# Step stores interleaved by blocks of four steps, a pipelined end of the forward loop, the last output gradients moved into the O projection, and the epilogue into the Wo gradient

## The chip, the cores and the metric

One core of one Trainium2 chip. The time is the device time of one execution in microseconds (us). Four executions of the kernel before agree within 0.3%. A ratio is the mean time of one kernel's fast runs over that of the other's fast runs of the same rounds, with a 95% interval; it is therefore not quite the ratio of the medians that stand beside it.

## The reference, cut to what matters

The kernel computes the value and all gradients of `x + s * g` in bfloat16, for 2048 tokens of width 640. `s` is a recurrent attention with 32 heads of 128: 64 steps of 32 tokens, each with 8 memory rows that are the output of the step before. `g` is the silu of a gated MLP.

```python
for s in range(n_seg):                       # 64 steps
    h = jnp.concatenate([mem, xs], axis=1)   # 8 memory rows and 32 token rows
    q, k, v = [jnp.einsum('btd,dhe->bhte', h, W) for W in (Wq, Wk, Wv)]
    p = _softmax(jnp.where(mask, scores(q, k), -1e9))
    o = jnp.einsum('bhte,hed->btd', jnp.einsum('bhqk,bhke->bhqe', p, v), Wo)
    mem = o[:, :M, :].copy()                 # the recurrence
...
return x + s * g                             # then jax.vjp of all of it
```

## The kernel before: the parts that the change and the argument touch

Only the 8 memory rows of a step hang on the step before. So the forward loop runs a chain of 64 steps on 32 or 40 rows, and puts the attention of whole *tiles* into its gaps: a tile is three steps' memory rows (24) and 96 token rows, 120 rows in all. A *unit* is one tile and four heads (512 columns). The backward loop is built the same way from the end. What a step computes for its rows (q, v, k, and in the backward loop gO) goes to a *step store* in DRAM, and tiles are loaded from there:

```python
self.QVS = mk("QVS", (T, 4, 32, 2, 1024))          # step, head group, row, q or v, column
self.KS  = mk("KS",  (T, 4, 32, 1024))
self.GOS = mk("GOS", (T, 4, 32, 1024))

def step_src(self, w, t0, t1, r0, r1, c0, c1):      # x rows: t1 - t0 = 4, r0:r1 = 8:32
    ...
    return XS[t0:t1, g, r0:r1, c0 - 1024 * g:c1 - 1024 * g]   # [4 steps, 24 rows, columns]
```

The first 672 token rows come from other stores (QVX, KX), whose rows are evenly spaced. The end of the forward loop, the tail, works off the units that are left when the chain has ended. It fills the gaps of steps that no longer exist:

```python
for t in range(T, 3 * k.NTL + 4):
    for g in ("W0", "W1", "W2", "G1", "G2", "G3", "G4", "G5", "G6"):
        FILL(g, t, ...)
```

After it come the O projection (with the fetch of three transposed weights, of copies QM of the memory rows, and the epilogue that makes out0 and gz), the last output gradients GX0 as a phase of their own, and the prologue of the backward loop. Each unit of the attention weight gradients, which follow the backward loop, makes eight loads:

```python
nc.sync.dma_start(dS[0:n, :, 0:n], k.DSR[tl][:, h0:h0 + 4, :])
nc.sync.dma_start(Pr[0:n, :, 0:n], k.PR[tl][:, h0:h0 + 4, :])
for nm_ in ("g", "q", "k"):
    k.load_x(r, nm, src, nc.scalar if nm_ == "g" else nc.sync)                       # 96 x rows
    (nc.sync if nm_ == "k" else nc.scalar).dma_start(r[0:nm, :], k.m_src(...))       # 24 memory rows
```

## Time and profile before

The median is 5976.96 us (three runs, 5975.18 to 5979.66).

| stage, from its tiles' starts and ends | us before |
|---|---|
| MLP forward and start | 619.3 |
| forward loop | 1340.9 |
| tail of the forward loop | 101.9 |
| O projection, then GX0, with the hand-overs | 207.9 |
| prologue of the backward loop | 107.8 |
| backward loop | 1304.7 |
| attention weight gradients, with their start | 1605.4 |
| load before the Wo gradient | 54.2 |
| Wo gradient | 176.4 |
| w2 gradient | 82.3 |
| rest of the MLP gradients | 377.8 |

The next rows are the kernel before's busy times in the long stretches: forward loop, backward loop, weight gradients, Wo gradient. The columns are the stretch, its length, busy time and instructions of each engine, the granted TensorE clock, the mean busy share of the 16 DMA engines, and GB/s.

```profile
core 0: us, PE busy (x) PEld busy (x) DVE busy (x) ACT busy (x) POOL busy (x), PEclk, DMA share, GB/s
620.00:1960.00 1340.00, 1211.98 (x22292) 733.70 (x22413) 744.67 (x2174) 699.11 (x2397) 526.15 (x733) 0.98 0.50 144
2378.00:3683.00 1305.00, 1136.69 (x24059) 756.15 (x24180) 588.80 (x2766) 380.47 (x1226) 408.36 (x747) 0.91 0.59 161
3710.00:5288.00 1578.00, 1441.79 (x11404) 927.96 (x11404) 446.30 (x958) 379.56 (x616) 0.00 (x0) 0.95 0.33 89
5342.00:5518.00 176.00, 175.97 (x1278) 125.94 (x1278) 13.42 (x30) 11.30 (x30) 0.00 (x0) 0.99 0.47 150
```

TensorE is idle for 128, 168 and 136 us in the three loops and not at all in the Wo gradient. No mean DMA share comes near 1 (0.33 to 0.59). The Pool is idle in the last two rows.

### The profile page before, as it was taken

Reading aid. Unit: us, or ns where it says so; the run is one execution under the profiler, and the core shown is the slowest. Engines: PE = TensorE matmul, PEld = TensorE weight load, DVE = VectorE, ACT = ScalarE, POOL = GpSimd, SP = SyncE. Lnnn points to the kernel's source line nnn. Section 1 sums busy time; section 2 is a strip of 40 time slices with the busy share of each in tenths; the row PEclk is TensorE's granted clock in tenths of the full one; section 3 lists DMA queues with packets and bytes.
Section 4 is the critical chain, followed back from the end, with each engine's and each line's share of the span. In section 5 each row is a group of like instructions: output and inputs, shape, how many; then the busy total and the mean of one; then the engine's idle time right before and its main releaser. Section 6 shows DMA issues by size and latency. Waiting matters only on the chain. (4 is left out here: it accounts for less than half of the span.)

```text
span 5978.5 us, 165521 instructions
## 1 busy us (share of the span) xinstructions
PE 5060.8 (85%) x67367; PEld 3238.0 (54%) x67644; DVE 2395.6 (40%) x7482; ACT 1840.4 (31%) x5059; POOL 1045.7 (17%) x1647
## 2 busy tenths in 40 slices
PE   5969799989988464888888886899999999969899
PEld 2546455555555242555555664665566556637565
DVE  5724455555555233444444442332233222300351
ACT  2424355555545212332222331221223222200110
POOL 0000244344444301333333331000000000000000
PEclk9979899999999686998889997999999999989999
DMA  6465355555444764665555664433233323353342
GB/s 222 160 249 195 102 154 155 148 149 150 146 138 142 217 191 118 158 171 165 160 164 166 181 175 108 108 83 84 76 96 89 89 79 86 101 204 122 106 123 92
DMA packets 999893, 839.75 MB, mean 140 GB/s; under 512 B 476653, under 2 KB 891561, under 8 KB 995817
## 3 DMA queue, kind: packets, MB, share of 16 engines
q1 hardware_dynamic: 771860, 580.65, 33.4%
q0 software_dynamic: 52080, 122.53, 7.1%
q10 hardware_dynamic: 175193, 125.97, 7.0%
q8 instruction: 533, 8.73, 0.6%
q14 instruction: 227, 1.86, 0.1%
HBM read 511.81 MB, written 327.01 MB: 140 GB/s over the span
## 5 line engine op out<-in xcount | busy, mean ns | idle before, releaser
L1405 PE MATMUL wg<-gr,hr 120*128 120x512 bf16 (+1 forms) x2640 | 592.9, 386 | 17.1 <-DVE dST L1337 12.6
L1383 PE MATMUL g<-w,gT 128*128 128x320 bf16 x3840 | 560.5, 304 | 0.0
L1383 PEld LDWEIGHTS <-gT 128*128 128x128 bf16 x3840 | 374.2, 99 | 143.4
L1405 PEld LDWEIGHTS <-hr 120*128 120x128 bf16 (+1 forms) x2640 | 258.7, 99 | 343.2 <-issue 51.8
L1773 POOL TENSOR_TENSOR o<-gxn,ln_G 128x640 bf16<-128x640 f32 x16 | 22.3, 1396 | 2130.9 <-DVE gxn L1771 2130.9
L366 PEld LDWEIGHTS <-gkv 128*8 128x8 bf16 x8192 | 213.3, 98 | 154.4 <-DVE gkv L1054 34.2
L90 DVE CAST wgo<-wg 128x512 bf16<-128x512 f32 x72 | 47.5, 688 | 588.1 <-PE wg L1405 315.6
L347 PEld LDWEIGHTS <-hx 128*32 128x32 bf16 x7680 | 178.0, 96 | 164.9 <-issue 5.1
L90 DVE CAST stg<-bank 128x512 bf16<-128x512 f32 x256 | 177.1, 692 | 200.6 <-PE bank L347 190.4
L1350 ACT CAST gr<-r6p 120x512 bf16<-120x512 f32 (+1 forms) x176 | 102.9, 585 | 495.0 <-PE r6p L1347 231.8
L366 PE MATMUL gbank<-WvT,gkv 128*8 128x320 bf16 x4096 | 227.6, 398 | 27.0 <-DVE gkv L1054 27.0
L652 ACT ACTIVATE xP<-xsp,xnm 120x120 bf16<-120x120 f32 (+1 forms) x704 | 239.8, 376 | 8.9 <-DMA PR<-xP 3.2
L1392 DVE TENSOR_TENSOR ghacc<-ghacc,g 128x320 f32<-128x320 f32 x240 | 117.0, 488 | 291.1 <-PE g L1383 291.1
L92 ACT CAST wgo<-wg 128x512 bf16<-128x512 f32 x48 | 25.8, 589 | 640.1 <-PE wg L1405 640.1
L1493 PE MATMUL oa<-gow,orr 128*128 128x320 bf16 x1280 | 176.4, 301 | 54.2 <-DMA gow<-GWO 54.2
L663 POOL TENSOR_TENSOR xP<-xP,xrz 120x480 bf16<-120x480 bf16 (+1 forms) x176 | 170.0, 966 | 162.8 <-ACT xP L652 95.6
L1189 DVE SCALAR_TENSOR_TENSOR gdS<-gdp,Dx,gPr 120x120 bf16<-120x120 f32 (+1 forms) x704 | 188.8, 331 | 0.0
L92 ACT COPY gT<-t6g 128x960 bf16<-128x960 bf16 (+5 forms) x216 | 167.2, 794 | 60.7 <-PE t6g L1366 59.3
L529 DVE COPY vt<-stg 8x512 bf16<-8x512 bf16 x512 | 162.8, 318 | 51.4 <-ACT stg L92 44.0
L1493 PEld LDWEIGHTS <-orr 128*128 128x128 bf16 x1280 | 126.1, 99 | 104.6 <-issue 54.6
L1161 POOL DMA_DIRECT2D VTD<-gvT x176 | 129.4, 736 | 289.0 <-ACT gvT L1160 265.1
L1186 DVE CUSTOM_DVE_ANT_0 gdS<-gdp,gPr 120x120 bf16<-120x120 f32 (+1 forms) x704 | 153.7, 274 | 59.5 <-PE gdp L1175 58.4
(326 smaller groups left out, 10716.3 us busy)
## 6 DMA issues: line engine op xcount, KB each, us to landing
QVS<-stg SPq DMA_DIRECT2D x128, 256.0 KB
gqv<-QVS SPq DMA_DIRECT2D x112, 192.0 KB
vTt<-VTD SPq DMA_DIRECT2D x64, 320.0 KB
orr<-OR SPq DMA_DIRECT2D x16, 1280.0 KB
OR<-xv POOLq DMA_DIRECT2D x168, 120.0 KB, 3.2
VTD<-gvT POOLq DMA_DIRECT2D x168, 120.0 KB, 4.6
PR<-xP POOLq DMA_DIRECT2D x168, 112.5 KB, 4.5
gPr<-PR SPq DMA_DIRECT2D x168, 112.5 KB
```

The lines of the kernel that those rows point to most:

```text
L90: return nc.vector.tensor_copy(out, in_)
L92: return nc.scalar.copy(out, in_)
L347: k.nc.tensor.matmul(bank[32 * g:32 * g + 32, :], x[:, dc, :], W[:, dc, c0:c0 + 512], start=(dc == 0), stop=(dc == k.DC - 1), tile_positio ...
L366: k.nc.tensor.matmul(pm[p0:p0 + nq, 0:320], x[:, h, :], W[:, h, 320 * b:320 * b + 320], start=(first and i == 0), stop=(last and i == 15), ...
L529: nc.vector.tensor_copy(vt[p0:p0 + 8, c0:c0 + 512], sv[32 * g:32 * g + 8, b * 512:(b + 1) * 512])
L652: nc.scalar.activation(Pb[0:n, j, 0:n], sp[0:n, j, :], ACT.Exp, bias=nmx[0:n, j:j + 1], scale=k.scale, accum_out=Z[0:n, j:j + 1])
L663: nc.gpsimd.tensor_tensor(Pb[0:n, :, 0:n], Pb[0:n, :, 0:n], bc_last(rz[0:n], n), ALU.mult)
L1186: nc.vector.tensor_tensor_reduce(dS[0:n, j, :], dp[0:n, j, :], Pr[0:n, j, :], 1.0, 0.0, ALU.mult, ALU.add, Dx[0:n, j:j + 1])
L1189: nc.vector.scalar_tensor_tensor(dS[0:n, j, :], dp[0:n, j, :], Dx[0:n, j:j + 1], Pr[0:n, j, :], op0=ALU.subtract, op1=ALU.mult)
L1383: nc.tensor.matmul(pg[:], ring[:, i, j, r0:r0 + P], Ws[qd][i][:, j, 320 * h:320 * h + 320], start=(i == 0 and j == 0), stop=(i == 2 and j ...
L1405: nc.tensor.matmul(accs[dc][:], hr[0:n, tl, dc * P:(dc + 1) * P], st["g", NTL * qd + tl, i][0:n, :], start=(tl == 0), stop=(tl == NTL - 1))
L1493: nc.tensor.matmul(ac[j][i][:], orr[:, w, jj * P:(jj + 1) * P], gow[:, w, 320 * i:320 * i + 320], start=(w == 0), stop=(w == NW - 1))
```

## The change

Its intent is to make the x rows of a tile one evenly spaced block of DRAM, so that their load keeps more DMA engines busy (in the kernel before, in stretches of the weight gradients in which hardly any packets but those of the step-store loads are in flight, such as 4761 to 4762 and 4766 to 4767 us, the DMA share is 0.26 and 0.27, about four of 16; it is 0.94 from 4757 to 4758, where the loads of dS and P run too); to take idle time out of the stretches between the loops; and to move what fills no gap there (the epilogue of out0) to where engines are idle. The memory rows of a tile now straddle blocks of four steps and are loaded in one or two pieces, in the weight gradients by the Pool. In the prologue, part of each unit's loads move to the ACT queue. Small copies out of the store FS move from the O projection into the backward loop.

```diff
-        self.QVS = mk("QVS", (T, 4, 32, 2, 1024))
+        self.QVS = mk("QVS", (T // 4, 4, 32, 4, 2, 1024))    # block of 4 steps, group, row, step in block, q or v, column
...                                                            (KS and GOS alike)
+    def blk_src(self, w, b, r0, r1, c0, c1):
+        XS = self.store(w)[b, :, 8:32]
...
+        XS = XS[g].rearrange("r t i c -> (r t) i c" if w == "qv" else "r t c -> (r t) c")[r0:r1]   # 96 even rows
+    def m_src(self, tl, w, c0, c1):
+        while t < end:
+            e = min(end, t - t % 4 + 4)                        # a piece ends where its block ends
...
@@ tail of the forward loop
-        for t in range(T, 3 * k.NTL + 4):
-            for g in ("W0", "W1", "W2", "G1", "G2", "G3", "G4", "G5", "G6"):
-                FILL(g, t, ...)
+        for i in range(len(tail) + 2):
+            for f, o in ((turn_q, 2), (lambda *u: ld("q", *u), 4), (scores, 1), (soft, 0),
+                         (lambda *u: norm(*u, nc.vector, nc.sync), 0), (turn_p, -1), (lambda *u: pv(*u, nc.scalar), -2),
+                         (lambda *u: ld("v", *u, nc.gpsimd), 1)):
+                if 0 <= i + o < len(tail):
+                    f(*tail[i + o])
@@ O projection
+            if fetch:
+                nc.sync.dma_start(*fetch.pop(0))               # weights: was Pool, two a turn, with four large QM copies
...
+            for _ in range(1 if b < 2 else 3):
+                if i >= 7 and g0:
+                    gox(*g0.pop(0))                            # GX0, was a phase of its own
-            (ep_ld, ep_b, ep_c, ep_d: the epilogue)           # now in the Wo gradient; QM: one copy a step of the forward loop
@@ prologue
+            if i % 3 == 1 and i < 12:
+                h0 = 8 * (i // 3)
+                nc.gpsimd.dma_start(WqT[:, h0:h0 + 8], ...)    # 4 x 1.25 MB, was one load ahead of GX0
+                ld(*todo.pop(0), nc.scalar if n0 > 0 else nc.sync)   # gO rows and probabilities of the prologue's units: ACT queue
@@ weight gradients
-                (nc.sync if nm_ == "k" else nc.scalar).dma_start(r[0:nm, :], k.m_src(tl, nm_, c0, c0 + 512))
+                k.load_m(r, tl, nm_, c0, c0 + 512, nc.gpsimd)
@@ Wo gradient
+                if tt + 1 < k.NT:
+                    ep_ld(tt + 1)                              # five loads of 128 rows, on the Pool queue
+                ep(tt)                                         # four DVE operations, out0 stored on the ACT queue
@@ w2 gradient
+                for tt in range(NT):                           # gz turned on TensorE; before, GZT was kept in DRAM
```

## The prediction

The marked cuts are rules and rates of the hardware that no trace of this case shows, and the estimates that rested on them. The sum came to -199 us (5778, put at 5780 us), and of its terms only 5 us of the O projection's 145 rest on a cut passage, which had the transfers of 18 MB take 52 us; at the 380 GB/s of the row 5291:5342 they take 47, as long as TensorE works there, so without the 5 the sum is -204. The -30, -40 and -18 of the even blocks come from measured intervals and steps. By "skew" the prediction means that a load whose rows are not evenly spaced keeps only a few DMA engines busy; the DMA shares above show this for the kernel before. Its 0.2 us of semaphores are two hand-overs; one, from the gz transposes to their copy, is 0.08 us in the kernel before. The prologue's 2.8 and 3.8 us a unit were not shown (the even gqv loads from QVX took 3.6 us to land in the kernel before, those from QVS 6.6).

> **What bounds the kernel now.** I read the page's slices first: the PE row stands at 8 or 9 tenths except in a few slices, so TensorE is the bound nearly everywhere and any gain has to come from the dips. I then cut the span into the kernel's stages (first and last start of each stage's tiles) and asked for busy time by stage:
>
> ```profile
> core 0: us, PE busy (x) PEld busy (x) DVE busy (x) ACT busy (x) POOL busy (x), PEclk, DMA share, GB/s
> 1960.00:2065.00 105.00, 28.65 (x321) 19.57 (x313) 16.17 (x63) 33.68 (x156) 43.78 (x64) 0.52 0.73 227
> 2065.00:2198.00 133.00, 83.28 (x1046) 69.15 (x1046) 59.16 (x148) 26.35 (x54) 1.74 (x1) 0.86 0.73 201
> 2198.00:2271.00 73.00, 54.16 (x240) 24.59 (x244) 16.56 (x24) 14.02 (x24) 0.00 (x0) 0.85 0.46 153
> 2271.00:2378.00 107.00, 28.13 (x456) 24.84 (x460) 33.97 (x242) 22.90 (x95) 23.66 (x42) 0.52 0.47 127
> 5291.00:5342.00 51.00, 0.00 (x0) 0.11 (x1) 0.05 (x1) 0.00 (x0) 0.00 (x0) 0.51 1.06 380
> 5519.00:5600.00 81.00, 64.65 (x448) 42.20 (x448) 7.52 (x17) 5.04 (x13) 0.00 (x0) 0.93 0.25 79
> ```
>
> The rows are: the tail of the forward loop, the O projection, the last output gradients (GX0), the backward prologue, the load before the Wo gradient, and the w2 gradient. The first four last 418 us and TensorE works 194 of them. The two long loops (forward 619 to 1960, backward 2378 to 3703) and the attention weight gradients (3703 to 5291) are 88 to 93% busy. Next the waits, in those stretches:
>
> ```profile
> PE xpo L698 <- DMA xv<-QVS: 40.4, 11, 9.1
> PE xpp L671 <- POOL xP L663: 25.7, 13, 3.4
> ...
> PE opt L840 <- DVE oT L90: 25.5, 15, 4.0
> ...
> PE gvpt L1157 <- DMA gqv<-QVS: 51.4, 18, 4.8
> PE gbank L347 <- POOL gox L1009: 19.3, 1, 19.3
> ...
> ACT stg L92 <- DMA KS<-stg: 31.6, 20, 3.6
> ```
>
> Two in the tail, one in the O projection, two in the prologue, one in the second half of the forward loop: loads from, and stores to, the step stores. Last the tile QVS, whose columns give issue time min/median/max in ns:
>
> ```profile
> L1141 SPq DMA_DIRECT2D gqv<-QVS x176: 650/758/917, 2213.9 to 3598.9; - x176
> L501 SPq DMA_DIRECT2D QVS<-stg x128: 319/344/1480, 626.8 to 1963.5; - x128
> L275 SPq DMA_DIRECT2D gqv<-QVS x128: 644/672/868, 2214.7 to 3182.1; - x128
> ```
>
> and the chain in the weight gradients, where seven loads of 4 to 5 us follow each other before TensorE goes on at one unit per 4.8 us:
>
> ```profile
> 4753.64 5.27 DMA r<-GOS
> 4758.93 5.32 DMA r<-GOS
> ...
> 4773.10 3.26 PE g L1383 x24
> ```
>
> A load from a step store takes 0.67 us or more to issue; a 128-partition store to the same tensor 0.34.
>
> [...] From the first WoT matmul of each step in the timeline, the 41 steps that load from QVS average 21.2 us with 24 us peaks, each peak with a 3 to 4 us wait on gqv<-QVS; the 22 that load the same bytes from QVX (96 even rows) average 19.8 with none. [...]
>
> **The change, part by part.**
>
> *Even blocks.* Stores put step t at [t//4, .., t%4], so 24 rows of 4 steps become 96 rows of one stride[...], same bytes. Weight gradients: [...] units there last 5.1 to 5.5. [...] From the starts of the g groups, 19 intervals sum to 97.8 us a pass (mean of 8), and would be 92.8 at the floor: 8 x 5.0 = 40. I take **-30**, since some early excess is ACT's, and -5 in the 53 us start of the stage. Backward loop: [...] Bringing 41 steps from 21.2 to the 20.2 of unstalled neighbours: **-40**. Forward loop: steps 25 on average 21.36 us against 20.62 before; the staging buffer waits for its KS store [...]. 38 x 0.73 = 28; I take **-18**, because the 64 QM copies move into this loop (about 0.7 us of Pool each, Pool 40% busy).
>
> *Added by the layout.* Memory rows of a tile now straddle blocks: 1 or 2 pieces (mean 1.5), twice that for qv. In the weight gradients 3 x 1.5 = 4.5 Pool issues x 0.7 us = 3.2 us per 4.8 us unit on an engine that was idle. In the backward loop SP gets about 6 more issues a step, some 4 us of 20; x loads get cheaper by 0.3 each. I count 0.
>
> *Tail.* 13 units. It is written in pipeline order, with norm on DVE (Pool took 990 ns) and v loads on Pool. ACT then bounds it: a large unit 4 x (381 + 227) + 571 + 586 = 3.6 us, a small one 4 x (288 + 203) + 295 + 578 = 2.8; 5 x 3.6 + 8 x 2.8 = 41, plus about 19 for the last step's leftovers, filling and draining = 60 instead of 105: **-45**. The weight fetches that ran at 227 GB/s in this stretch also leave it.
>
> *O projection with GX0.* TensorE: 83.3 - 9.0 (gz transposes, gone) + 54.2 = 128.5 us. But 14 MB of weights now come in here with 3.8 MB of OR rows in the first 13 units: [...] With 5 for that and 11 for start and end: 145 instead of 206, which had an 18.6 us hand-over between the stages: **-61**.
>
> *Prologue.* 19 units. DMA latency bounds them (5.4 us each); loads become even and are split over two queues: 8 x 2.8 + 11 x 3.8 = 64, start 10, hand-over to the loop 13 (was 19.3): 87 for 107, **-20**. WqT (5 MB) now loads in it.
>
> *Epilogue into the Wo gradient.* Five loads and four DVE ops of about 0.5 us per 128 rows, 16 x 2 = 32 us on a DVE that is 8% busy: hidden. gz (2.6 MB) leaves the saturated 51 us and two sets of ep loads enter: -3. But gz is now turned on TensorE: 16 x (5 transposes 0.5 + copy 0.66 + semaphores 0.2) in one PSUM buffer = +22 before the w2 gradient, +5 for w1T and w3T, whose loads must now wait for that memory; the GZT loads leave the last blocks, -4: **+20**.
>
> Sum: -30 - 5 - 40 - 18 - 45 - 61 - 20 + 20 = -199. 5977 - 199 = 5778; I say **5780 us**.
>
> **Rivals.** (1) The loops' stalls are SP's order, not engine skew: SP waits 68 us in 800 for the krow buffer (PE gbank L1112). Then even rows buy nothing in the loops: -93 falls away, 5870. Against it: the QVX steps have the same krow waits (66 us in 440) and no stall. (2) The split memory rows take over as the wait: SP or Pool issue[...]. I give it +20 to +40: 5810. Lookahead of 3 to 4 units speaks against it. (3) The merged phase is DMA-bound, as the fetch that was hidden under the slow tail is now in it: 165 to 175 instead of 145: 5805. It speaks for this that the old O projection already moved 201 GB/s. (4) Better than thought: forward and backward loops at their unstalled 20 us throughout, the weight gradients at their floor: a further -40, 5740.
>
> **Range and chances.** The tail, merged phase and prologue rest on idle TensorE that is plain to see (224 us); I have half of it. Of the rest 93 hangs on the skew reading. 8 in 10: 5715 to 5850. Faster by over 2% needs 5857; even rival (1) alone misses it narrowly, so 0.92 faster, 0.07 same, 0.01 slower.
>
> **What would show it.** Tail about 60 us with ACT near full; merged phase 145 us at PE over 85%; no gvpt wait on gqv<-QVS in the backward loop and steps near 20 us; issue times of x-row loads near 0.35 us; weight-gradient units at 4.8 us throughout; about 20 us more before the w2 gradient. I am wrong if the loops keep their 24 us steps, if TensorE waits on memory-row loads (KS, GOS, QVS from Pool), or if the merged phase waits on orow or WoT for tens of us.

## The result, and the profile after

The changed kernel takes 5744.07 us (median of four runs, 5724.69 to 5751.58), against 5978.31 for four runs of the kernel before: a ratio of 0.9601 (0.9575 to 0.9627). The profiled spans are 5978.5 and 5743.5 us, 235.0 apart, and the stages add up to that:

| stage | before | after | difference | predicted |
|---|---|---|---|---|
| MLP forward and start | 619.3 | 622.2 | +2.9 | 0 |
| forward loop | 1340.9 | 1301.3 | -39.6 | -18 |
| tail | 101.9 | 53.7 | -48.2 | -45 |
| O projection and GX0 | 207.9 | 139.7 | -68.2 | -61 |
| prologue | 107.8 | 107.3 | -0.5 | -20 |
| backward loop | 1304.7 | 1267.3 | -37.4 | -40 |
| weight gradients | 1605.4 | 1535.4 | -70.0 | -35 |
| load before the Wo gradient | 54.2 | 53.8 | -0.4 | -3 |
| Wo gradient | 176.4 | 197.9 | +21.5 | 0 |
| w2 gradient | 82.3 | 81.8 | -0.5 | +27 |
| rest | 377.8 | 383.2 | +5.4 | -4 |

Here are the same rows for the changed kernel: forward loop, tail, O projection with GX0, prologue, backward loop, weight gradients, load, Wo gradient, w2 gradient.

```profile
core 0: us, PE busy (x) PEld busy (x) DVE busy (x) ACT busy (x) POOL busy (x), PEclk, DMA share, GB/s
622.00:1924.00 1302.00, 1194.38 (x22308) 722.79 (x22432) 746.38 (x2178) 703.92 (x2403) 554.23 (x784) 0.99 0.54 151
1924.00:1977.00 53.00, 27.11 (x300) 19.18 (x299) 20.34 (x74) 32.38 (x151) 21.53 (x36) 0.56 0.40 80
1983.00:2117.00 134.00, 122.51 (x1165) 79.69 (x1172) 35.19 (x84) 28.88 (x55) 0.00 (x0) 0.97 0.76 214
2117.00:2224.00 107.00, 28.51 (x461) 25.26 (x459) 33.89 (x243) 22.83 (x96) 27.15 (x45) 0.52 0.60 176
2224.00:3491.00 1267.00, 1130.91 (x24051) 749.51 (x24176) 589.21 (x2765) 378.31 (x1226) 417.77 (x760) 0.92 0.63 168
3522.00:5027.00 1505.00, 1410.21 (x11404) 915.10 (x11403) 445.57 (x958) 382.57 (x616) 419.53 (x760) 0.96 0.38 93
5027.00:5081.00 54.00, 0.39 (x2) 0.28 (x3) 6.89 (x14) 0.24 (x1) 11.81 (x22) 0.52 1.03 369
5081.00:5279.00 198.00, 180.54 (x1280) 127.27 (x1277) 39.34 (x84) 12.08 (x32) 30.88 (x58) 0.96 0.56 181
5279.00:5360.00 81.00, 70.40 (x528) 46.66 (x528) 11.03 (x25) 10.68 (x21) 0.00 (x0) 0.98 0.34 110
```

In the tail TensorE still works its 27 us, but the stretch is half as long and moves 80 GB/s where it moved 227. The O projection with GX0 has TensorE busy 91% of the time, and TensorE again runs at nearly its full clock in it. The prologue row is hardly changed from the one in the prediction: the same length, 28 us of TensorE, half the clock. The Wo gradient, where TensorE had no idle time before, now has 17 us of it.

The issue times of the x-row loads from QVS in the changed kernel, as minimum/median/maximum in ns ahead of the span of times:

```profile
L282 SPq DMA_DIRECT2D xq<-QVS x120: 307/410/933, 1104.0 to 1961.4; - x120
L282 SPq DMA_DIRECT2D gqv<-QVS x120: 544/605/684, 2120.9 to 2990.0; - x120
L282 SPq DMA_DIRECT2D r<-QVS x120: 317/401/1438, 3560.9 to 4933.1; - x120
```

The first and the last are loads of 96 rows of 1 KB, whose medians were 626 and 652 ns before. The load of gqv moves twice as many rows, and its median fell only from 672 to 605 ns. So most of the length of this issue, which the prediction took as a sign of skew, was the number of rows. In the backward loop, no step lasts over 23 us (from the first WoT matmul of a step to that of the next); nine did before. In that loop of the kernel before, TensorE waits for gqv (us in total, times, longest):

```profile
PE gvpt L1157 <- DMA gqv<-QVS: 39.7, 17, 6.5
```

The changed kernel has no such row in its loop. In the weight gradients, which work in eight passes of 20 units, 19 intervals between the starts of the g groups sum to 91.1 us in six of the eight passes; in the kernel before they sum to 96.2 to 98.4 us in seven passes.

Last, the ACT queue in the load before the Wo gradient of the changed kernel (start, duration of the issue, number of issues):

```profile
5026.86 12.41 ACTq L1706 DMA_DIRECT2D hb_all<-HB  x4
5060.20 0.37 ACTq L1708 DMA_DIRECT2D w2T<-W2T  x1
5060.61 9.25 ACTq L1506 DMA_DIRECT2D gow<-GWO  x2
5069.95 9.35 ACTq L1491 DMA_DIRECT2D out_dram<-ep_g  x2
```

TensorE waits for gow until 5080.6. Gow is issued behind 9 MB for the w2 stage, which starts 200 us later. That was so in the kernel before, too (54.2 us); the change did not touch it. The trace shows a second reason for the delay: from 5039.3 to 5060.2 the ACT queue issued nothing. w2T is counted on the same semaphore as SP's load of orr before it. That load was issued at 5028.65 and landed at 5060.18, and w2T was issued at 5060.20.

### The profile page after: what moved, and what is told of

Its sections match the earlier page's. It is cut to its first block, busy times and chain, and to the rows that moved or that the text cites. A ratio compares the mean times of both kernels' runs of the same rounds, so it can differ in the third digit from the quotient of the medians.

```text
span 5743.5 us, 166838 instructions
## 1 busy us (share of the span) xinstructions
PE 5004.5 (87%) x67332; PEld 3202.8 (56%) x67614; DVE 2395.4 (42%) x7479; ACT 1838.9 (32%) x5045; POOL 1530.8 (27%) x2536
## 5 line engine op out<-in xcount | busy, mean ns | idle before, releaser
L1385 PE MATMUL g<-w,gT 128*128 128x320 bf16 x3840 | 547.5, 299 | 0.0
L250 POOL DMA_DIRECT2D r<-GOS x256 | 143.0, 561 | 925.3 <-PE r6p L1349 876.3
L1185 POOL DMA_DIRECT2D DSR<-gdS x176 | 100.9, 573 | 412.1 <-DVE gdS L1183 391.1
L712 POOL DMA_DIRECT2D OR<-xv x163 | 94.8, 582 | 404.7 <-ACT xv L711 284.9
L674 POOL TENSOR_TENSOR xP<-xP,xrz 120x480 bf16<-120x480 bf16 x163 | 161.9, 994 | 140.1 <-ACT xP L663 90.9
L1518 PEld LDWEIGHTS <-orr 128*128 128x128 bf16 x1280 | 127.5, 100 | 124.4 <-issue 72.3
```

Of the source, the lines that this page charges most:

```text
L250: eng.dma_start(d, src if src.shape[0] > 1 else src[0])
L674: eng.tensor_tensor(Pb[0:n, :, 0:n], Pb[0:n, :, 0:n], bc_last(rz[0:n], n), ALU.mult)
L1385: nc.tensor.matmul(pg[:], ring[:, i, j, r0:r0 + P], Ws[qd][i][:, j, 320 * h:320 * h + 320], start=(i == 0 and j == 0), stop=(i == 2 and j ...
L1518: nc.tensor.matmul(ac[j][i][:], orr[:, w, jj * P:(jj + 1) * P], gow[:, w, 320 * i:320 * i + 320], start=(w == 0), stop=(w == NW - 1))
```

## The experiments

Twelve kernels were run. Stage times are from their traces, the ratios from their rounds; the kernel before was rerun in each group, and chips differ by up to 0.3% in its median.

### 1. Are the even rows what pays in the loops?

In the changed kernel, the x-row loads were made to read 24 rows from each of the four head groups, instead of 96 even rows from one. The values are wrong; bytes, queues and order are the same.

```diff
-        XS = XS[g].rearrange("... -> (r t) i c" or "(r t) c")[r0:r1]
+        XS = XS[:, 0:r1 // 16].rearrange("... -> g (r t) i c" or "g (r t) c")     # slowest dimension 4, not 96
```

> The changed kernel, with only the source address of its x-row loads altered: the same bytes in the same queues and order, but read as 4 runs of 24 rows from four places of the step store instead of one run of 96 evenly spaced rows (the values are wrong on purpose). Stores, memory-row loads and all else stay. Theory [...]: the gain of the loops goes back. Issue times of x-row loads from the step stores return from about 0.35 to 0.65 us or more; forward loop +20 to +40 us from its 1301, backward loop +30 to +40 from its 1267, weight gradients +35 to +70 from their 1535; total 5830 to 5890. Rival (the loops gained because the memory rows and QM copies left the busy SP and ACT queues and the order of issue changed; the shape of the loads is worth nothing): every stage within 5 us of the changed kernel, total 5735 to 5760.

Measured: 5871.79 us, ratio to before 0.9837 (0.9823 to 0.9852), by median 128 us slower than the changed kernel. The issue times returned (that of gqv only from 605 to 679 ns):

```profile
L283 SPq DMA_DIRECT2D xq<-QVS x120: 611/627/732, 1101.4 to 1990.8; - x120
L283 SPq DMA_DIRECT2D gqv<-QVS x120: 625/679/717, 2150.5 to 3105.9; - x120
```

and in its backward loop TensorE waits for them again (us in total, times, longest):

```profile
PE gvpt L1152 <- DMA gqv<-QVS: 60.1, 19, 7.1
```

(What was tested is whether the shape of the loads is what paid.) The kept traces tell the two shapes apart in a second way, by the number of increments that a load's semaphore gets while the load lands. For the gqv loads from QVS in the backward loop it is 16 in the changed kernel, and 5 in the skewed kernel and the kernel before; for those from QVX in the kernel before, whose rows are even, it is 16. From its issue, the gqv load from QVS takes 3.1 us to land in the changed kernel, 5.4 in the skewed one and 6.6 in the kernel before, where that from QVX, of the same bytes, takes 3.6 (medians). By stage: forward loop +30, prologue +14, backward loop +75, weight gradients +3. So the theory holds in the two loops, twice as strongly as predicted in the backward one, and the rival of the queues' order falls there. In the weight gradients it fails: skewed loads cost next to nothing there.

### 2. A square for the weight gradients

The other thing that changed in that stage is the memory rows: the Pool issues them, in one or two pieces. One kernel put them back on SP and ACT, another did that and the skewed loads together.

```diff
-                k.load_m(r, tl, nm_, c0, c0 + 512, nc.gpsimd)
+                k.load_m(r, tl, nm_, c0, c0 + 512, nc.sync if nm_ == "k" else nc.scalar)
```

> The changed kernel, with the memory-row loads of the attention weight gradients put back from the Pool queue to the queues that they had in the kernel before (ACT for g and q, SP for k). That stage gained 70 us where the prediction had 35. Theory (the excess is ACT's and SP's issue time, taken off by the move to Pool): the stage gets 25 to 40 us longer (1560 to 1575 for 1535), because the memory rows now straddle blocks and are 1.5 issues each, total 5770 to 5785. Rival (the even x rows alone carry the 70): the stage stays within 8 us, total 5740 to 5755. No other stage moves.

> Both edits together, for the fourth corner of the square. If the two effects in the weight gradients simply add, the stage is longer than in the changed kernel by the sum of what the two single edits cost. If either alone lets the loads keep ahead of TensorE (a unit has 4.8 us), the single edits cost little and both together cost the whole 70 us or more: the stage at 1605 or above, total 5850 to 5920.

Measured, from the first matmul of the stage to its last, in us (before: 1577):

| | memory rows on Pool | memory rows on SP and ACT |
|---|---|---|
| x rows even | 1505 (5744.07 in all) | 1544 (5779.64, ratio 0.9677) |
| x rows skewed | 1508 (5871.79) | 1665 (6030.5, ratio 1.0100) |

The two do not add: 3 and 39 alone, 160 together. (From the end of the backward loop, as in the stage table, the 39 are 35, because the start of the stage is 4 us longer with the Pool.) The second expectation of the corner came true, and by more than the whole gain. The corner is not the kernel before, which also has skewed x rows and memory rows on SP and ACT, but these in one piece, and is 88 us faster in this stage. No run tells whether the split makes these 88 us, or that the skewed rows come from four head groups instead of four steps. In the corner, ACT's copies of the results stand behind late loads (wait in total, times, longest):

```profile
ACT gr L1353 <- DMA r<-QVS: 114.4, 26, 6.7
ACT gr L1353 <- DMA r<-GOS: 97.8, 31, 6.2
```

With the memory rows on the Pool, those two lines of the waits vanish (0.8 us is left of them in the changed kernel), whatever the shape of the x rows. In the corner, 19 intervals sum to 107.5 us a pass (mean of 8), 5.7 each. And even x rows with memory rows on SP and ACT still lose 19 us in the passes and 12 in the start, so the shape of the x rows is not the whole cause.

The kept traces hold an account that fits all of this. In this stage SP and ACT count their transfers on the same eight semaphores, and an issue there waits until the transfer that used its semaphore last has landed. Where the Pool issues the memory rows, they are counted on eight other semaphores. The table gives the loads of a unit on SP and ACT, the median time from issue to landing of ACT's x-row load from GOS, the time for which ACT's queue stood idle ahead of a load, and the stage:

| kernel | loads a unit | to landing | ACT idle ahead of loads | stage |
|---|---|---|---|---|
| before | 8 | 4.7 us | 180 us | 1577 us |
| changed | 5 | 3.2 us | 29 us | 1505 us |
| skewed, memory rows on Pool | 5 | 4.6 us | 29 us | 1508 us |
| even, memory rows on SP and ACT | 9.4 | 2.6 us | 164 us | 1544 us |
| skewed, memory rows on SP and ACT | 9.4 | 4.0 us | 248 us | 1665 us |

All but 1 us of the idle time in each row ended when the transfer on the load's own semaphore had landed. So in these kernels a skewed load costs little as long as nothing waits for its semaphore (3 us with 5 loads a unit), and with 8 or 9.4 loads a unit something does. This puts all five stages in order. It also explains the chain of loads that the prediction shows, each of which starts as the one before lands (4753.64 + 5.27 = 4758.91, and the next starts at 4758.93). No run changed the number of semaphores, so this account is read from the traces and not tested; what sets the landing time itself stays open.

### 3. The split memory rows, in the loops

The skewed kernel's backward loop, 1342.7 us, is 38 us longer than that of the kernel before, which has skewed x rows as well, but memory rows in one piece. So the skewed kernel was run with memory rows in one piece (again wrong values).

```diff
-            e = min(end, t - t % 4 + 4)
-            XS = self.store(w)[t // 4, g, 0:8, t % 4:t % 4 + e - t]
+            e = end
+            XS = self.store(w)[t // 4, g, 0:8, 0:e - t]
```

> The run with skewed x-row loads (4 runs of 24 rows), and in addition each tile's memory rows read as one whole piece from the block of the tile's first step (wrong values on purpose), in place of 1 or 2 pieces. This gives the loads of the loops the shape that they had in the kernel before, while all else is the changed kernel. That run's backward loop took 1342.7 us, 38 more than the kernel before. Theory (the split of the memory rows costs about 38 us where the x rows are skewed; in the changed kernel the even rows hide it): backward loop 1295 to 1315, forward loop 1320 to 1335, total 5815 to 5840. Rival (the 38 us have another cause, for instance that the four runs come from four places): backward loop 1330 or more.

Measured: 5850.07 us, ratio 0.9772 (0.9750 to 0.9793). The backward loop takes 1323.0 us, between the two expectations; the forward loop is as before this edit (1330.9). So the split of the pieces costs about 20 us of the 38 where x rows are skewed; the other 18 are open. No run has even x rows and memory rows in one piece, so what the split costs in the changed kernel was not measured; there is no wait for gqv left in it.

### 4. The tail alone, and the tail with the fetch moved

The kernel before was given the tail of the changed kernel and nothing else.

```diff
@@ the kernel before
+        tail = ...;  for i in range(len(tail) + 2): ...     # the loop of the change, on the old stores
```

> The kernel before, with only the tail of its forward loop rewritten in the pipelined order (norm on DVE, its store on SP, output-row store and v loads as in the changed kernel). The step stores keep their old layout, and the weight fetches and the QM copies still run in this stretch. Theory (the tail was short because of its order alone): tail 102 to 50-60 us, total 5978 to 5925-5935. Rival (it also needed the even rows and the weight fetches out of its way): tail 70 to 85 us, total 5945 to 5965, and what is gained in the tail may be given back in the O projection, which then starts before its weights are there.

Measured: 5968.49 us, ratio 0.9989 (0.9967 to 1.0011): nothing. The tail took 91.0 us, only 11 less, and the hand-over to the O projection 19.5 instead of 7.0. The rival is nearer, though it had the tail at 70 to 85. What the kernel's DMA issues list between 1960 and 2078 us shows (size, median us from issue to landing):

```profile
WoT<-WOT POOLq DMA_DIRECT2D x5, 1024.0 KB, 8.5
WvT<-WVT POOLq DMA_DIRECT2D x4, 1280.0 KB, 10.5
QM<-QVS POOLq DMA_DIRECT2D x4, 1024.0 KB, 17.2
```

The Pool has nothing to do at this point, so the weight fetches of the next phase run as soon as the old weights' memory is free, in the tail, on the queue that now also carries the tail's v loads. The next kernel moved them:

```diff
@@ the kernel before with the new tail, O projection
-            for _ in range(2):
-                if i >= 2 and fetch:
-                    nc.gpsimd.dma_start(*fetch.pop(0))
+            if fetch:
+                nc.sync.dma_start(*fetch.pop(0))
```

> The kernel before with the pipelined tail, as in the run that did only that, and one thing more: the 13 weight fetches and the 4 QM copies, which in that run were issued on the Pool queue and moved 20 MB in the tail, are now issued on SP inside the O projection, one per turn. Theory (the pipelined tail gained only 11 of 48 us because its loads shared the DMA engines and the Pool queue with those fetches): tail 91 to 52-58 us, hand-over to the O projection 19.5 to 6-8 us; the O projection then has to bring the weights itself and gets 0 to 15 us longer (from 202); total 5925 to 5945. Rival (the old layout of the step stores keeps the tail slow): tail still 75 us or more, total above 5955. The run with the skewed loads in the changed kernel, whose tail was 56.3 us, already speaks against the rival.

Measured: tail 57.6 us and hand-over 7.1, as the theory said; but 6008.2 us in all, ratio 1.0035 (1.0013 to 1.0057). The O projection with GX0 went from 201 to 272 us, 55 more than the upper end of the expectation. TensorE waits for its rows in it:

```profile
PE opt L858 <- DMA orow<-OR: 61.4, 18, 7.6
```

The fetch that left the slow stage was paid for in the next one. The change differs there in four ways, which were not tested singly: GX0's matmuls fill the O projection, the epilogue with its loads and stores has left it, five row buffers replace three, and the QM copies went to the forward loop. The -48 and the -68 of the table have to be counted together.

### 5. The Wo gradient

First, the stores of out0 were moved from ACT's queue to the Pool's; then, in another kernel, each epilogue step was written after the evictions of its half block.

```diff
-            nc.scalar.dma_start(out0f[tt * P:tt * P + P, :], g)
+            nc.gpsimd.dma_start(out0f[tt * P:tt * P + P, :], g)
```

> The changed kernel, with the stores of out0 in the Wo gradient put on the Pool queue instead of ACT's; all else as it is. The Wo gradient went from 176 to 198 us when the epilogue moved into it. Theory (four of the out0 issues hold ACT for about 14 us each, as they wait for DVE's result and that for a load, and ACT's half of the evictions of the Wo gradient stands behind them): the stage falls to 178 to 184 us, total 5725 to 5732. Rival (DVE's own epilogue operations, which wait for the ep loads ahead of DVE's half of the evictions, hold TensorE as much): 190 to 198 us, total 5738 to 5745. No other stage moves.

```diff
-                ep(tt)
                 b = 4 * jp
                 ...
                     nc.sync.dma_start(out6f[hh * P:(hh + 1) * P, :], ot[:])
+                ep(tt)
```

> The changed kernel, with each epilogue step of the Wo gradient written after the matmuls and evictions of its half block instead of before them; queues unchanged. Now no eviction of the same half block stands behind a wait for the ep loads on either ACT or DVE. Theory (ACT or DVE waiting for ep loads ahead of evictions is what costs 21 us): 178 to 184 us, and the first w2 matmul is not later after it than now (73.7 us for the w2 stage, up to 76 since the last epilogue ends later). Rival (the loss is the lower clock, 0.96 for 0.99, and the added traffic): 190 us or more.

Measured: 5740.13 us (0.9602) and 5742.77 us (0.9615), neither to be told from 0.9601. With the stores on Pool the stage is 13 us shorter, 184.7, close to the theory's 178 to 184; but the load before it is 13 longer, 67.0 instead of 53.8, and the sum is 251.7 in both. With the steps written last the stage is unchanged to 0.1 us. What TensorE waits for in the stage of the changed kernel, beyond gow, is DVE's evictions:

```profile
PE oa L1518 <- DVE wgoo L1523: 15.1, 3, 8.5
```

It is 14.9 us where the steps are written last, and 0.2 with the stores on Pool. DVE itself waits there for the epilogue's loads (21.5 us in 11 waits for ep_s). The writes of gz suggest why the new order in the text changed nothing. This phase is not kept to its written order, and nothing holds the epilogue back but its own buffers: in the changed kernel its 16 steps run from 10.7 to 127.5 us after the end of the weight gradients, four of them in the load and the rest in the first 74 us of the Wo gradient. They are no later where they are written last (11.0 to 127.3). With the stores on Pool they run still earlier, from 10.9 to 101.8, nine of them in the load, which is 13 us longer. The epilogue moves 16 MB in all (six streams of 2.6), and what runs early shares the queues and the DMA engines with gow and the first OR blocks: in the changed kernel 20 MB move in the load (369 GB/s for 54 us).

So a third kernel wrote the phase in order, each engine kept to it: gow and the first rows first, the 9 MB for the next stage one piece per block, the next block's rows ahead of the block, out0's store on Pool.

```diff
+        o_ld(0)                       # OR rows of block 0 on SP, gow on ACT
+        ep_ld(0)
         for qd in range(8):
+            if qd + 1 < 8:
+                o_ld(qd + 1)
+            if fetch:
+                nc.scalar.dma_start(*fetch.pop(0))      # hb in four pieces, then w2T: were ahead of gow
             ...
+        in_order(k, start)
```

> The changed kernel, with the Wo gradient written in order: gow and the first half blocks of OR are issued first, the four hb loads and w2T (9 MB, ahead of gow on the ACT queue until now) one per block after that, the next block of OR before the block's matmuls, out0's store on Pool, and each engine kept to the written order, so that the epilogue advances one 128-row step per half block instead of as early as its buffers allow. Theory (in the changed kernel TensorE waits 54 us for gow because 9 MB stand ahead of it, and the 21 us more in the stage come from the epilogue's loads running in the first third of it, where they delay the OR blocks and ACT): load before the Wo gradient 54 to 22-32 us, the stage 198 to 176-186, w2 stage within 5 us of 73.7; total 5744 to 5695-5712. Rival (the 15.7 MB of epilogue traffic cost their 20 us wherever they run, and the load is a matter of all bytes of the stage): 5725 or more.

Measured: 5694.1 us, ratio 0.9510 (0.9489 to 0.9532).

```profile
core 0: us, PE busy (x) PEld busy (x) DVE busy (x) ACT busy (x) POOL busy (x), PEclk, DMA share, GB/s
5028.00:5052.00 24.00, 0.47 (x3) 0.08 (x2) 3.60 (x7) 0.88 (x2) 8.59 (x16) 0.53 1.00 337
5052.00:5233.00 181.00, 178.06 (x1280) 126.69 (x1280) 40.25 (x91) 11.49 (x31) 42.57 (x80) 0.98 0.79 263
```

The load takes 23.5 us instead of 53.8 (TensorE's wait is now for orr, the first OR rows), there is no wait for DVE's evictions left, and the stage 181.2 instead of 197.9, while it moves 263 GB/s instead of 181. The epilogue's steps now come one every 10.9 us. So 17 of the 21 us went with the written order, and the epilogue's bytes cost at most 5. The run changes several things together; it does not part the pacing of the epilogue from the order of the loads, nor from the stores on Pool.

### 6. The prologue

Two kernels tested what holds it at 107 us. The first moves each turn's memory gradients, and with them the load that reuses their buffers, ahead of the transposes, and the GXP stores off SP; the second issues WqT at the end of the prologue.

```diff
-            for f, o in ((turn, 0), (dprob, 1), (dsoft, 1), (gmem_ld, 2)):
+            for f, o in ((dprob, 1), (gmem_ld, 2), (turn, 0), (dsoft, 1)):
-            nc.sync.dma_start(k.GXP[tl, :, qd, 0:ns], ...)
+            (nc.gpsimd if (tl, qd) in pro else nc.sync).dma_start(k.GXP[tl, :, qd, 0:ns], ...)
```

> The changed kernel, with two edits in the prologue of the backward loop: in each turn the memory-gradient matmuls of the unit two back, and the load that reuses its buffers, come before the transposes of this turn's unit instead of after them, and the GXP stores of the prologue's units go to the Pool queue instead of SP. Theory (the prologue is a loop of load, transposes, copies, store, next load, with two units in flight per load latency, because a load is issued only once the unit that waits for the load before it has been turned): the prologue, 107.3 us from the end of GX0 to the first loop step, falls to 80 to 90 us; total 5720 to 5730. Rival (the WqT loads, 5 MB in the same stretch, or the memory rows' issue time set its length): 100 us or more, total within 8 us of 5744.

```diff
-            if i % 3 == 1 and i < 12:
-                h0 = 8 * (i // 3)
+            for h0 in range(0, H if i == len(pro) - 2 else 0, 8):
                 nc.gpsimd.dma_start(WqT[:, h0:h0 + 8], ...)
```

> The changed kernel, with the four WqT loads of the prologue all issued near its end (turn 17) instead of in turns 1, 4, 7 and 10, where the prologue's own loads run. Theory (the loop of load and reuse sets the prologue's length): 100 us or more for it, and as much lost again at the first step of the loop if WqT is late. Rival (the 5 MB in the way of the prologue's loads set it): 85 to 92 us, with 5 to 10 us given back where the loop waits for WqT. Total within 10 us of 5744 under the theory, 5725 to 5735 under the rival.

Measured: reordered, 5716.22 us, ratio 0.9573 (0.9557 to 0.9590); WqT late, 5732.32 us, ratio 0.9598 (0.9580 to 0.9616), which is the changed kernel's. Reordered, the prologue takes 96.3 us. That is 11 less, below the rival's figure but above the theory's 80 to 90; the run does not part the new order from the move of the GXP stores. The two fences give TensorE's waits in it, of the changed kernel and of the reordered one:

```profile
PE gvpt L1151 <- DMA gqv<-QVS: 42.8, 14, 8.8
```

```profile
PE gvpt L1151 <- DMA gqv<-QVS: 7.4, 3, 3.9
PE gdp L1168 <- ACT gOT L1160: 38.2, 19, 7.1
```

The old wait is gone, and most of its time returned under another name, at ACT's copies. With WqT late, TensorE still waits 37.8 us for gqv, but the last unit of the prologue starts 70.6 us after the end of GX0 instead of 85.2, and yet the loop starts at 105.4. TensorE waits 29.4 us at its start for the gox copy (16.6 in the changed kernel): the load for that copy, gride, is the last on SP, behind the loads of the loop's first units, and those now run beside WqT. So both play a part: the loop of load and reuse, and 5 MB in its way. (The reordered kernel's backward loop was also 12 us shorter, 1255; in the other kernels with even rows it takes 1259 to 1272, so that is hardly more than its scatter.)

### 7. A version that beats both

> A version to beat both: the changed kernel with the written order in the Wo gradient (as in the run sent beside this one), the reordered prologue (which alone gave 17 us by ratio), and WqT fetched right after the last use of Wo, ahead of the prologue instead of within it. If the gains add: prologue 107.3 to 78-90 us, Wo gradient with its load 252 to 205-215 us, total 5660 to 5690. If the prologue's loads now wait behind WqT at its start, 5685 to 5710.

It joins the written order in the Wo gradient, the reordered prologue, and WqT fetched right after the last use of Wo. Measured: 5683.66 us (five runs, 5673.85 to 5688.37), ratio 0.9489 (0.9469 to 0.9508); correct. The prologue takes 90.4 us and the Wo gradient with its load 204.9; the total is in the upper part of the first range. In the prologue, WqT now delays the first unit instead: TensorE waits 14.1 us for gPr at its start. Against the changed kernel's ratio this is 1.2% less. The prologue's gain came only in part on top of the written order's: the two ratios are 0.9489 and 0.9510, with intervals that overlap.

## Why the prediction was right or wrong

The total of 5780 us was 36 too high, and inside its range. That it came so near is in part luck: by stage, the change gained 95 us more than predicted in five places (weight gradients 35, w2 stage 28, forward loop 22, O projection 7, tail 3) and 59 less in the others (Wo gradient 22, prologue 20, the rest 17). By its steps:

- **Even blocks, backward loop (-40 predicted, -37).** Right in cause, and in size by the sum of two terms. The even rows are worth 56 to 75 us (the two skewed kernels against the changed one), and 18 us that stay open go the other way (the skewed kernel with memory rows in one piece against the kernel before). "I count 0" for the split of the memory rows stands as far as the waits show; where the x rows are skewed the split costs 20. One piece of the evidence was misread: the issue of gqv took 672 ns, but an even one takes 605.
- **Even blocks, forward loop (-18 predicted, -40).** The cause was right, the term too small. The prediction worked out 28 from the late steps and took 18, because the QM copies come into the loop. Skewing the rows alone costs 30; the copies showed no cost, since the loop of the skewed kernel, which has them, is still 10 us shorter than that of the kernel before (a difference that no run took apart).
- **Even blocks, weight gradients (-30 - 5 predicted, -70).** The term was half of what was measured, and the attribution was incomplete. The failed sentence is the one on the Pool, "on an engine that was idle", with the sum "I count 0": moving the memory rows to the Pool is worth 35 to 39 us by itself, and makes the shape of the x rows worth 3 us in this stage. And what held the units was, by the traces, a wait of the loads for their semaphores (ACT's queue idle for 180 us before, 29 after), and not the long landing of the loads alone (read from the traces, not tested; experiment 2). The predicted floor, 4.8 us per unit, is where it now runs, but 19 intervals of it are 91.2 us, and not the prediction's 92.8: its own figures give 53 us for the eight passes where it wrote 40 and took 30. The passes gained 53.
- **Tail (-45, measured -48) and O projection with GX0 (-61, measured -68).** Both sums were right to 7 us, but the tail's reason was not: the prediction gave it to ACT-bound pipelining, with the fetches as an aside. On the kernel before, the pipelining alone gained 11 us in the tail and nothing in all. Nor is ACT near full in the new tail, as it was to be: it is busy 32 of 53 us.
- **Prologue (-20 predicted, -0.5).** This step failed: "loads become even and are split over two queues: 8 x 2.8 + 11 x 3.8 = 64". It took the interval per unit from the loads' lengths, when it also hung on the order in which a load is issued, behind the unit that waits for an earlier one: with another order, and the GXP stores off SP, it is 11 us shorter. The even rows did help, 14 us by the skewed kernel, and WqT in the same stretch may have taken that back (the last unit starts 15 us earlier without it).
- **Epilogue into the Wo gradient ("hidden", measured +21).** The step counted DVE's busy time, 32 us, and left out that in a phase not kept to its order this work runs as early as its buffers allow. In the written order it is nearly hidden (+5).
- **End of the kernel (+27 - 4 predicted for the w2 and MLP gradients, +5 measured).** The gz transposes were expected in one block ahead of the w2 matmuls. They run among them: the w2 stage is 0.5 us shorter than before.
- **Slips that changed little.** The backward loop is 87% busy, not 88. The mean of the eight passes before is 98.3 us; 97.8 is about their median. The weights fetched in the O projection are 15.7 MB (13 loads of 1.0 or 1.3), not 14.
- **Rivals.** Rival 1, SP's order instead of skew, falls in the two loops; by chance, the kernel with skewed rows takes 5872 us, very near the 5870 that it named. Rival 2, the split rows, is no wait in the changed kernel's backward loop. Rival 3, a DMA-bound merged phase, falls: it takes 140 us with the hand-over, and in 134 of them TensorE is busy 91%. Rival 4 came nearest, with 5740: the weight gradients are at the floor that it named, and no step of the backward loop stalls; but the forward and backward steps average 20.4 and 20.1 us, and the prologue and the Wo gradient took back part of the rest.

## What to carry to other kernels

Lay a store out so that the rows of a large load are evenly spaced, and judge the load by its time from issue to landing (5.4 against 3.1 us here), not by the mean DMA share. Where the rows cannot be even, moving other small loads to an idle queue can be worth as much: here 157 us with skewed rows (1665 to 1508), and 39 with even ones (1544 to 1505). Count the transfers in flight against the semaphores that count them: with 8 loads a unit on eight semaphores ACT's queue stood idle for 180 us of 1577, with 5 for 29 of 1505. Work taken out of a slow stage may have been hidden there: test a stage's rewrite on the old kernel, and count it only together with the stage that now pays. Where an engine waits for a transfer, read first what stands ahead of it in its queue, and what the queue itself waits for: writing the end in order took 30 us off the load before the Wo gradient.
